# Hourglass attention with a GELU feed-forward layer: from batch 3 on, each head's 64 features on 64 partitions for the scores

## The chip, the cores and the metric

The kernel runs on one core of a Trainium2 chip. The metric is the device time of one execution in microseconds (us); lower is better. The time before the change is the median of three runs. The trace comes from one further, profiled execution.

The engines are named as in the profile: PE is TensorE (matrix products, with PEld for its weight loads), DVE is VectorE, ACT is ScalarE, POOL is GpSimd, SP is SyncE, whose queue here issues transfers only.

## The reference

Inputs `q`, `k`, `v` have the shape (8 batches, 8 heads, 576 tokens, 64 features); `w_in` is 512 x 2048 and `w_out` 2048 x 512. All are float32, and so is the output of 4608 x 512.

```python
# attention: B, H, S, D = 8, 8, 576, 64; factor = 4; Sd = 144
q_d, k_d, v_d = means over 4 neighbouring tokens          # (B, H, Sd, D)
out_d = softmax(q_d @ k_d.T / sqrt(D)) @ v_d
out_up = np.repeat(out_d, 4, axis=2)
mask = np.abs(pos[:, None] - pos[None, :]) < 4             # a band of 7 tokens
scores = np.where(mask, q @ k.T / sqrt(D), -1e9)
out_local = softmax(scores) @ v
x = (out_up + out_local).transpose(0, 2, 1, 3).reshape(B * S, H * D)
# feed-forward layer
h = x @ w_in
g = h * (1.0 / (1.0 + np.exp(-1.702 * h)))
return (g @ w_out).astype(np.float32)
```

## The kernel before, in words

**Two interleaved programs.** The feed-forward layer works on nine groups of 512 tokens. For group `g`, `mm1` makes 16 blocks of 128 hidden features (`hps_mm`, L712, four matmuls of 512 columns each) and ACT applies Silu to each (L723). `mm2` makes four blocks of 128 tokens by 512 outputs (L776, 16 matmuls each), ACT copies each into an `osb` buffer (L761) and SP stores it (L766). Batch `b = g + 1` goes through attention while group `g` runs; batch 0 is done before the groups, and groups 7 and 8 have no attention beside them.

**Positions.** The order of all engines is written out by hand. `attention(b)` returns six steps, and `POS = [13, 16, 35, 45, 56, 69]` says ahead of which block of `mm1` (0 to 15) or matmul of `mm2` (16 to 79, counted on from 16) each is put into the program. The steps are, for batches 2 to 7: the first scores on PE (13), their exponentials and masks (16), the second scores with exponentials and masks (35), the products with the values for head pairs 0 and 1 with their normalisation (`avn(0, 1)`, 45), `av_tr` (the same for pairs 2 and 3, and pair 0 turned back and merged, 56), and `tr(1, 2, 3)` (the other pairs turned back and merged, 69).

**Heads.** The eight heads are two quads `qd` (four heads) and four head pairs `hp`. One transfer per quad and name brings k or q as bfloat16 into `kb`, `qb` (L185, issued by POOL, two buffers each): head `r` of the quad lies on partitions 32r to 32r+31, 18 tokens to a partition. `prep_1` (L262) turns it on DVE in 32x32 blocks of 4-byte words, that is, of pairs of features: in `kT`, `qT` head `r` keeps its 32 partitions, and the pair's two features lie side by side in the last index `a`. A dot product over 64 features is thus two matmuls over 32 partitions, `a = 0` and `a = 1`, summed in PSUM.

**Scores.** `scores_mixed` makes the local scores in blocks of 64 keys by 60 queries: five chunks `i`, two halves `par`, four heads, two `a`, that is 80 matmuls (`score`, L360). The scores of the means (`score_d`, L372) are 24 matmuls of 144 columns. Their operands `kdT`, `qdT` are sums over four tokens that POOL makes in two steps (`pool_qk`, L292 and L296). ACT takes the exponentials (`exp_local` L410, `exp_down` L416), and DVE multiplies the local ones by the band's mask (`mask_local`, L424). `mask_local` comes behind the batch's preparation in DVE's order, and in the same order as the steps.

**Values.** SP loads the values twice, as rows (`load_v` into `vf`, one buffer) and as groups of four rows (`load_v4` into `v4`, one buffer). POOL casts the first (`prep_v`, L302) and sums the second (`prep_v4`, L308 and L311). The results `vbs` and `vds` have two buffers, one for odd and one for even batches.

**After the scores.** `av` makes 40 matmuls for a head pair (`av_local` L441 with 64x64 tiles, `av_down` L463), `normalise` divides by the sums on DVE (L479, L480), `transp` turns the result on PE (L494, L504), ACT spreads the part of the means (`copy_od`, L618), and DVE adds both into `xT` (`merge`, L639 and L645). The next group's first matmuls read `xT`.

**PSUM.** Three tiles `PA` go round: a score stage takes three, `avn(0, 1)` two, `av_tr` three, `tr(1, 2, 3)` three; the next group's first block takes one. Two tiles `PM` serve the feed-forward layer.

**Preparation.** At the head of each group, L904 to L935 put the work for batch `b` on the queues. For groups 1 to 6 that is, on DVE, four transposes; on POOL, the sums of quad 0, the loads of batch `b + 1`'s k and q, the cast of the values, the sums of quad 1, and the sums of the values; on SP, `load_v4(b)` and `load_v(b + 1)`.

Of the kernel before, what the change touches and what calls it, by code (L numbers as in the profile page):

```python
# [19 lines left out]
def kernel(  # L20
# [43 lines left out]
    eds = [persist.tile([128, 2, 480], BF16, name=f"ed{i}") for i in range(2)]  # L64
    v4 = persist.tile([128, 3, HP, 4 * D], FP32, name="v4")
    kdT = [persist.tile([128, 160, 2], BF16, name=f"kdT{i}") for i in range(NQ)]

    PA = [psum.tile([128, 2, 512], FP32, name=f"pa{i}") for i in range(3)]
    PM = [psum.tile([128, 512], FP32, name=f"pm{i}") for i in range(2)]
# [10 lines left out]
        return PM[turn["m"] % 2]  # L80

    wz = consts.tile([128, 512], BF16, name="wz")
    wf = consts.tile([128, 512], FP32, name="wf")
    off = consts.tile([128, 60], BF16, name="off")
    psel = consts.tile([128, 7, 64], BF16, name="psel")

# [24 lines left out]
    def fill():  # L111
        nc.vector.memset(wz, 0.0)
        nc.vector.memset(wf, 0.0)
        for t in kdT:
            nc.vector.memset(t[:, SD:160, :], 0.0)
        for t in vbs:
            nc.vector.memset(t[:, :, :, 64:65], 1.0)
        for t in vds:
            nc.vector.memset(t[:, :, :, 64:65], 4.0)
        for t in es:  # L120
            nc.vector.memset(t[:, :, 300:304], 1.0)
        for t in eds:
            nc.vector.memset(t[:, :, 432:480], 1.0)
# [56 lines left out]

    def load_1(name, src, store, b, qd):
        t = ldp.tile(
            [128, 1152], BF16, name=f"{name}b{qd}", tag=f"{name}b{qd}", bufs=2
        )
        nc.gpsimd.dma_start(  # L185
            out=t,
            in_=bass.AP(
                tensor=src.tensor, offset=src[b, 4 * qd].offset,
                ap=[[1152, 128], [1, 1152]],
            ),  # L190
        )
        store[b, qd] = t
# [75 lines left out]
    def prep_qk(b, qd):  # L268
        prep_1("k", b, qd)
        prep_1("q", b, qd)  # L270

    def new_qdT(b, qd):
        t = work.tile([128, SD, 2], BF16, name=f"qdT{qd}", tag=f"qdT{qd}", bufs=1)
# [115 lines left out]
    def scores_d(b, qd, sd):  # L389
# [3 lines left out]
                    score_d(b, qd, sd, kc, a, r)  # L393
        return sd

    def scores_mixed(b, qd):
        sp, sd = [ps_tile(), ps_tile()], ps_tile()
        for i in range(5):
            for a in range(2):
                if i >= 2:  # L400
                    for r in range(4):
                        score_d(b, qd, sd, i - 2, a, r)
                for x in (1, 0):
                    for r in range(4):
                        score(b, qd, sp, i, a, r % 2 if x == 0 else 1 - r % 2, r)
        return sp, sd
# [254 lines left out]
    def attention(b, slots=None):  # L661
        st = {}

        def s_pe(qd):
            st["s", qd], st["d", qd] = scores_mixed(b, qd)

        def s_act(qd):
            if qd == 0:
                nc.scalar.preload_act_table_set("exp_and_others")
            exp_local(qd, st["s", qd])  # L670
            exp_down(qd, st["d", qd])
            if qd == 1:
                nc.scalar.preload_act_table_set("silu_and_others")
            mask_local(qd)

        def s1():
            s_pe(1)
            s_act(1)

        def avn(*hps):  # L680
            def f():
                for hp in hps:
                    st["o", hp] = av(b, hp, slots and slots[hp % 2])
                for hp in hps:
# [24 lines left out]
        return first + [av_tr, tr(1, 2, 3)]  # L709

    def hps_mm(g, ffc, dmc, acc):
# [190 lines left out]
    for g in range(n_groups):  # L902
        b = g + 1
        if g == 0:  # L904
# [14 lines left out]
            nc.gpsimd.memset(v4[32:64], 0.0)  # L919
            load_v(2, gate=after(w_out_bf[0:1, 12, 0:1], nc.gpsimd))  # L920
            load_v4(2)
        elif b < B:
            if b > 2:
                load_v4(b)
            prep_qk(b, 0)
            pool_qk(b, 0)
            if b + 1 < B:
                for qd in range(NQ):
                    load_qk(b + 1, qd)
            prep_v(b, nc.gpsimd)  # L930
            if b + 1 < B:
                load_v(b + 1)
            prep_qk(b, 1)
            pool_qk(b, 1)
            prep_v4(b, nc.gpsimd)  # L935
        steps = {}
        if b < B:
            for n, f in zip(POS if g else POS_0, attention(b, None if g else (1, 2))):
# [36 lines left out]
```

## Time and profile before

| What | Value |
|---|---|
| Time, median of 3 runs | 323.0 us (322.31 to 323.63) |
| Time of the profiled execution | 320.42 us |
| Its span, first to last instruction | 318.6 us |
| Granted TensorE clock | 1.00 |
| Matmuls of the feed-forward layer, L712 and L776, busy | 139.2 and 128.7 us |
| Matmuls of the scores, L360 and L372 | 1280 of 197 ns and 384 of 230 ns |
| Weight loads of the scores, L360 | 1280 of 104 ns |
| DVE, transposes L262 | 32, 39.8 us |
| POOL, sums L292 and L296 of one name and quad | 1.15 and 0.67 us |
| POOL, one step of the value sums L308 and L311 | 1.33 and 0.76 us |
| DVE waiting for ACT ahead of the masks | 89.1 us in 14 places, the longest 12.6 us |
| POOL waiting for DVE's transposes | 84.7 us in 6 places, the longest 15.8 us |

The span is what the trace holds; the profiled execution's own time has 1.8 us around it. A duration in the trace is that of one instruction, and matmuls overlap: what a stage of matmuls takes is read from where it begins and where the next stage begins. A wait of an engine that is not the bound costs nothing by itself.

The order of POOL's and DVE's work in the group that begins at 128.24 us, with times from the span's start: DVE ends the merges of batch 3 at 129.07 and turns k and q until 133.5; POOL's sums run from 130.32, its four load issues from 134.00, the cast from 136.13, and the sums of the values from 142.15 to 148.6. The first scores begin on PE at 139.55, the second at 147.45, and the first products with the values at 150.69; the last step ends at 158.71, and the next group begins at 161.10.

### The profile page before, as it was taken

What the parts mean: (1) busy time and instruction counts of PE and PEld (TensorE: products, weight loads), DVE (VectorE), ACT (ScalarE), POOL (GpSimd) and SP (SyncE); (2) the same over time, 40 slices, a digit from 0 to 9 for tenths busy, and PEclk for the clock granted to TensorE, in tenths of its full rate; (3) what the DMA queues carried; (4) which work ended last, traced back from release to release, by engine and by line L of the source; (5) the groups of instructions that cost most, each with busy time, mean ns of one, the idle gap of its engine ahead of it and who ended that gap; (6) DMA issues with size and microseconds to landing.
All of it is one profiled execution on the core that took longest, in us unless ns stands there. A gap on an engine that the chain in (4) does not pass through costs nothing.

```text
span 318.6 us, 10993 instructions
## 1 busy us (share of the span) xinstructions
PE 309.5 (97%) x4927; PEld 156.9 (49%) x4927; DVE 133.6 (42%) x222; ACT 184.0 (58%) x314; POOL 138.9 (44%) x168
## 2 busy tenths in 40 slices
PE   7899999999999989999999999999999999999995
PEld 4465455444554545455545554455445544444444
DVE  6963825730684066703780378027811650000000
ACT  4464773577647674658465846674667556415611
POOL 8843782099209930696049703980297000000000
PEclk9999999999999999999999999999999999999999
DMA  7999999999719941598259915991360110020011
GB/s 121 116 191 209 184 90 207 185 270 230 180 39 218 199 114 70 144 216 173 71 134 206 188 41 136 206 205 58 109 107 2 71 68 2 0 99 33 2 65 67
DMA packets 64078, 40.02 MB, mean 126 GB/s; under 512 B 44064, under 2 KB 55456, under 8 KB 64032
## 3 DMA queue, kind: packets, MB, share of 16 engines
q0 software_dynamic: 19392, 14.95, 33.3%
q1 hardware_dynamic: 44496, 24.32, 32.7%
q8 instruction: 38, 0.62, 0.9%
q10 hardware_dynamic: 144, 0.07, 0.1%
q14 instruction: 8, 0.07, 0.1%
HBM read 44.83 MB, written 9.44 MB: 170 GB/s over the span
## 4 chain that ended last, share of the span: by engine, by line
PE 86%; DMA 7%; POOL 4%; issue 1%; ACT 0%; DVE 0%; POOLq 0%
PE pm L776 37%; PE pm L712 33%; DMA kb<-in_k_dram 5%; PE pa L360 3%; PE pa L776 2%; DMA qb<-in_q_dram 2%; PE pa L441 2%; PE pa L712 2%; PE pa L494 2%; PE pa L372 2%; PE pa L463 2%; PE pm L791 1%; POOL w_in_bf L238 1%; POOL vb L216 1%; POOL pq L292 1%
## 5 line engine op out<-in xcount | busy, mean ns | idle before, releaser
L776 PE MATMUL pm<-w_out_bf,gT 128*128 128x512 bf16 x528 | 120.8, 380 | 0.4 <-issue 0.4
L712 PE MATMUL pm<-xT,w_in_bf 128*128 128x512 bf16 x512 | 119.2, 379 | 0.0
L723 ACT ACTIVATE gT<-pm 128x512 bf16<-128x512 f32 x128 | 76.3, 598 | 44.7 <-PE pm L712 44.7
L712 PEld LDWEIGHTS <-w_in_bf 128*128 128x128 bf16 x576 | 55.6, 98 | 66.2
L776 PEld LDWEIGHTS <-gT 128*128 128x128 bf16 x560 | 52.0, 98 | 60.8 <-issue 1.7
L424 DVE TENSOR_TENSOR es<-es,mask 128x600 bf16<-128x600 bf16 x28 | 18.6, 667 | 90.1 <-ACT es L410 89.1
L292 POOL TENSOR_TENSOR pq<-kT 128x576 f32<-128x576 bf16 x13 | 15.1, 1159 | 84.7 <-DVE kT L262 84.7
L761 ACT ACTIVATE osb<-pm 128x512 f32<-128x512 f32 (+2 forms) x35 | 20.5, 586 | 38.3 <-PE pm L776 34.2
L618 ACT COPY od<-pa 128x384 f32<-128x384 f32 (+1 forms) x56 | 19.0, 406 | 26.4 <-PE pa L504 23.3
L480 DVE TENSOR_TENSOR y<-pa,rc 128x896 bf16<-128x896 f32 x28 | 30.6, 1092 | 1.0
L410 ACT ACTIVATE es<-pa 128x600 bf16<-128x600 f32 x32 | 19.7, 668 | 10.8 <-PE pa L360 10.6
L639 DVE TENSOR_TENSOR xT<-pa,od 128x570 bf16<-128x570 f32 x28 | 21.0, 752 | 8.0 <-ACT od L618 8.0
L308 POOL TENSOR_TENSOR v<-v 112x512 f32<-112x512 f32 x18 | 23.9, 1330 | 0.0
L763 DVE TENSOR_SCALAR osb<-pm 128x128 f32<-128x128 f32 x1 | 0.3, 293 | 55.0 <-ACT osb L761 55.0
L262 DVE STREAM_TRANSPOSE kT<-kb 128x576 f32<-128x576 f32 x16 | 20.0, 1248 | 5.6 <-DMA kb<-in_k_dram 5.5
L262 DVE STREAM_TRANSPOSE qT<-qb 128x576 f32<-128x576 f32 x16 | 19.8, 1240 | 0.8 <-DMA qb<-in_q_dram 0.6
L712 PE MATMUL pa<-xT,w_in_bf 128*128 128x512 bf16 x64 | 20.0, 379 | 0.0
L360 PEld LDWEIGHTS <-kT 32*64 32x64 bf16 x1280 | 14.7, 104 | 7.8 <-issue 6.6
L360 PE MATMUL pa<-qT,kT 32*64 32x60 bf16 x1280 | 17.2, 198 | 1.3 <-DVE qT L262 1.3
L216 POOL DMA_DIRECT2D vb<-in_v_dram x20 | 13.7, 699 | 8.1 <-DMA w_in_bf<-in_moe_w_in_dram 3.6
L292 POOL TENSOR_TENSOR pq<-qT 128x576 f32<-128x576 bf16 x13 | 14.9, 1147 | 0.0
L416 ACT ACTIVATE ed<-pa 128x864 bf16<-128x864 f32 x16 | 14.3, 897 | 0.1
(92 smaller groups left out, 278.9 us busy)
## 6 DMA issues: line engine op xcount, KB each, us to landing
out_dram<-osb SPq DMA_DIRECT2D x35, 256.0 KB, 2.1
vf<-in_v_dram SPq DMA_DIRECT2D x60, 128.0 KB, 5.3
v<-in_v_dram SPq DMA_DIRECT2D x36, 192.0 KB, 4.5
kb<-in_k_dram POOLq DMA_DIRECT2D x16, 288.0 KB, 6.5
qb<-in_q_dram POOLq DMA_DIRECT2D x16, 288.0 KB, 7.9
w_in_bf<-in_moe_w_in_dram POOLq DMA_DIRECT2D x4, 512.0 KB, 12.1
w_out_bf<-in_moe_w_out_dram POOLq DMA_DIRECT2D x4, 512.0 KB, 8.7
vb<-in_v_dram POOLq DMA_DIRECT2D x20, 64.0 KB, 5.7
```

Source lines behind the costliest of these rows:

```text
L262: nc.vector.transpose(out=t32.rearrange("p (i c) -> p c i", c=18), in_=store[b, qd].bitcast(FP32).rearrange("p (c d) -> p c d", c=18),)
L292: nc.gpsimd.tensor_tensor(out=t1, in0=sv[:, :, 0:2, :], in1=sv[:, :, 2:4, :], op=ALU.add)
L308: eng.tensor_tensor(out=t1[0:112], in0=x[:, :, 0:2, :], in1=x[:, :, 2:4, :], op=ALU.add)
L360: nc.tensor.matmul(sp[r // 2][64 * par : 64 * par + 64, r % 2, 60 * i : 60 * i + 60], lhsT=kT[b, qd][rows, k0 : k0 + 64, a], rhs=qT[b, qd] ...
L410: nc.scalar.activation(out=es[2 * qd + u][:, :, 0:300], in_=sp[u][:, :, 0:300], func=AF.Exp, scale=inv_sqrt_d,)
L480: nc.vector.tensor_tensor(out=y[:, xs], in0=ov[:, :, :, 0:D], in1=rc[:, xs].to_broadcast([128, n, 7, D]), op=ALU.mult,)
L618: nc.scalar.copy(out=od[:, 4 * t0 : 4 * (t0 + n)].rearrange("p (t f) -> p t f", f=4), in_=x[:, xx, 288 : 288 + n, None].to_broadcast([128, ...
L639: eng.tensor_tensor(out=sub(xT[hp], t0 + 3, (57, 2), (114, 5), (1, 57)), in0=sub(x, 3, (509, 2), (57, 5), (1, 57)), in1=sub(od, 3, (57, 2) ...
L712: nc.tensor.matmul(acc, lhsT=w_in_bf[:, dmc, ffc * 128 : (ffc + 1) * 128], rhs=xT[dmc][:, g * TG : g * TG + TG], start=(dmc == 0), stop=(d ...
L723: nc.scalar.activation(out=gT[:, ffc, :], in_=acc, func=AF.Silu, scale=GELU_SCALE)
L761: eng.activation(out=osb, in_=ap, func=AF.Copy, scale=1.0 / GELU_SCALE)
L776: nc.tensor.matmul(ops[t], lhsT=gT[:, ffc, t * 128 : (t + 1) * 128], rhs=w_out_bf[:, ffc, :], start=(ffc == 0), stop=(ffc == n_ffc - 1),)
```

## The change

From batch 3 on (`WIDE = 3`), the scores use a different layout. `turn2` turns k or q in 32x32 blocks of 2-byte elements, so that features 0 to 31 and 32 to 63 of a head lie in two planes `a` on the same 32 partitions. `widen` then moves 32-partition blocks with five copies on DVE: one saves plane 1 of all heads, and four put the two planes of each head onto 64 adjacent partitions (heads 0 and 2 of a quad in plane 0, heads 1 and 3 in plane 1). `pool_wide` sums over four tokens on POOL as before. `scores_wide` makes the scores with one matmul over 64 partitions in place of two over 32: 40 local ones and 12 of the means for each quad.

`attention` of these batches has `avn(0, 1)` ahead of the second scores, with its own positions `POS_W`. At the head of the groups, the values of batches 3 to 7 are prepared one batch ahead on POOL, and SP loads them first; `prep_wide` puts the transposes, the copies, the sums and the loads of the next batch's k and q in turn. In group 1 (batch 2), the cast and the sums of the values go from POOL to DVE, the loads of quad 1 for batch 3 come behind quad 1's transposes, and the values of batch 3 are prepared on POOL at the end.

The loads of k and q have one buffer in place of two, for all batches, and the constant `wf` lies in `v4`, which is not yet in use at that point.

```diff
+    kdW = [persist.tile([128, 2, 160], BF16, name=f"kdW{i}") for i in range(NQ)]
+    qdW = [persist.tile([128, 2, SD], BF16, name=f"qdW{i}") for i in range(NQ)]
+    kW = [persist.tile([128, 2, S], BF16, name=f"kW{i}") for i in range(NQ)]
+    qW = [persist.tile([128, 2, S], BF16, name=f"qW{i}") for i in range(NQ)]
+    WIDE = 3
...
-    wf = consts.tile([128, 512], FP32, name="wf")
+    wf = v4.rearrange("p k h c -> p (k h c)")[:, 0:512]
...
+        for t in kdW:
+            nc.vector.memset(t[:, :, SD:160], 0.0)
...
-            [128, 1152], BF16, name=f"{name}b{qd}", tag=f"{name}b{qd}", bufs=2
+            [128, 1152], BF16, name=f"{name}b{qd}", tag=f"{name}b{qd}", bufs=1
...
+    def turn2(name, b, qd):
+        store, dst = (kf, kW) if name == "k" else (qf, qW)
+        nc.vector.transpose(
+            out=dst[qd].rearrange("p a (i c) -> p c a i", c=18),
+            in_=store[b, qd].rearrange("p (c a d) -> p c a d", c=18, a=2),
+        )
+
+    def widen(name, b, qd):
+        w = (kW if name == "k" else qW)[qd]
+        half = work.tile([128, S], BF16, name="half", tag="half", bufs=1)
+        nc.vector.tensor_copy(out=half, in_=w[:, 1, :])
+        for s in range(2):
+            lo, hi = slice(64 * s, 64 * s + 32), slice(64 * s + 32, 64 * s + 64)
+            nc.vector.tensor_copy(out=w[lo, 1, :], in_=w[hi, 0, :])
+            nc.vector.tensor_copy(out=w[hi, 0, :], in_=half[lo, :])
+
+    def pool_wide(name, qd):
+        src, dst = (kW[qd], kdW[qd][:, :, 0:SD]) if name == "k" else (qW[qd], qdW[qd])
+        sv = src.rearrange("p x (j f) -> p (x j) f", f=4)
+        t1 = work.tile([128, 2, SD, 2], FP32, name="pq", tag="pq")
+        nc.gpsimd.tensor_tensor(
+            out=t1.rearrange("p x j f -> p (x j) f"),
+            in0=sv[:, :, 0:2], in1=sv[:, :, 2:4], op=ALU.add,
+        )
+        nc.gpsimd.tensor_tensor(
+            out=dst, in0=t1[:, :, :, 0], in1=t1[:, :, :, 1], op=ALU.add
+        )
+
+    def prep_wide(b):
+        def turn_load(name, qd):
+            turn2(name, b, qd)
+            if b + 1 < B:
+                load_1(name, *((k, kf) if name == "k" else (q, qf)), b + 1, qd)
+
+        def finish(name, qd):
+            widen(name, b, qd)
+            pool_wide(name, qd)
+
+        turn_load("k", 0)
+        finish("k", 0)
+        turn_load("q", 0)
+        turn_load("k", 1)
+        finish("q", 0)
+        turn_load("q", 1)
+        finish("k", 1)
+        finish("q", 1)
...
+    def scores_wide(qd):
+        sp, sd = [ps_tile(), ps_tile()], ps_tile()
+        for i in range(5):
+            for x in range(2):
+                for s in range(2):
+                    rows = slice(64 * s, 64 * s + 64)
+                    for par in range(2):
+                        k0 = 114 * i + KSTART[par]
+                        q0 = 114 * i + QSTART[par]
+                        nc.tensor.matmul(
+                            sp[s][64 * par : 64 * par + 64, x, 60 * i : 60 * i + 60],
+                            lhsT=kW[qd][rows, x, k0 : k0 + 64],
+                            rhs=qW[qd][rows, x, q0 : q0 + 60],
+                            start=True, stop=True,
+                            tile_position=(64 * s, 64 * par),
+                        )
+            if 1 <= i < 4:
+                kc = i - 1
+                for s in range(2):
+                    rows = slice(64 * s, 64 * s + 64)
+                    for x in range(2):
+                        nc.tensor.matmul(
+                            sd[64 * x : 64 * x + 64, s, SD * kc : SD * kc + SD],
+                            lhsT=kdW[qd][rows, x, 48 * kc : 48 * kc + 64],
+                            rhs=qdW[qd][rows, x, :],
+                            start=True, stop=True,
+                            tile_position=(64 * s, 64 * x),
+                        )
+        return sp, sd
+
     def scores_mixed(b, qd):
+        if b >= WIDE:
+            return scores_wide(qd)
...
+        if b >= WIDE:
+            first = first[:2] + [avn(0, 1), s1]
         return first + [av_tr, tr(1, 2, 3)]
...
     POS = [13, 16, 35, 45, 56, 69]
+    POS_W = [13, 16, 35, 46, 59, 71]
...
-        elif b < B:
-            if b > 2:
-                load_v4(b)
+        elif b < WIDE:
             prep_qk(b, 0)
             pool_qk(b, 0)
-            if b + 1 < B:
-                for qd in range(NQ):
-                    load_qk(b + 1, qd)
-            prep_v(b, nc.gpsimd)
+            load_qk(b + 1, 0)
+            prep_qk(b, 1)
+            load_qk(b + 1, 1)
+            prep_v(b, nc.vector)
+            load_v(b + 1)
+            prep_v4(b, nc.vector)
+            load_v4(b + 1)
+            pool_qk(b, 1)
+            if b + 1 == WIDE:
+                prep_v(b + 1, nc.gpsimd)
+                prep_v4(b + 1, nc.gpsimd)
+        elif b < B:
             if b + 1 < B:
                 load_v(b + 1)
-            prep_qk(b, 1)
-            pool_qk(b, 1)
-            prep_v4(b, nc.gpsimd)
+                load_v4(b + 1)
+            prep_wide(b)
+            if b + 1 < B:
+                prep_v(b + 1, nc.gpsimd)
+                prep_v4(b + 1, nc.gpsimd)
```

The step lists take `POS_W` in place of `POS` from batch 3 on.

More of the change, by code (lines that the diff above doesn't have):

```diff
@@ L921 @@
             load_v4(2)
-        elif b < B:
-            if b > 2:
-                load_v4(b)
+        elif b < WIDE:
             prep_qk(b, 0)
             pool_qk(b, 0)
-            if b + 1 < B:
-                for qd in range(NQ):
-                    load_qk(b + 1, qd)
-            prep_v(b, nc.gpsimd)
+            load_qk(b + 1, 0)
[10 more added lines that the diff above has]
+        elif b < B:
             if b + 1 < B:
                 load_v(b + 1)
-            prep_qk(b, 1)
-            pool_qk(b, 1)
-            prep_v4(b, nc.gpsimd)
+                load_v4(b + 1)
[3 more added lines that the diff above has]
+                prep_v4(b + 1, nc.gpsimd)
         steps = {}
         if b < B:
-            for n, f in zip(POS if g else POS_0, attention(b, None if g else (1, 2))):
+            for n, f in zip(POS_W if b >= WIDE else POS if g else POS_0, attention(b, None if g else (1, 2))):
                 steps.setdefault(n, []).append(f)
```

## The prediction

> **What bounds the kernel now.** I read the engines' busy time and the chain of waits first, then the windows of one group with attention and one without.
>
> ```profile
> PE 309.5 (97%) x4927; PEld 156.9 (49%) x4927; DVE 133.6 (42%) x222; ACT 184.0 (58%) x314; POOL 138.9 (44%) x168
> ...
> PE 86%; DMA 7%; POOL 4%; issue 1%; ACT 0%; DVE 0%; POOLq 0%
> ...
> 128.24:161.10 32.86, 32.86 (x602) 16.59 (x601) 15.90 (x25) 21.02 (x36) 17.75 (x19) 1.00 0.67 147
> ...
> 260.00:287.60 27.60, 27.60 (x130) 12.52 (x129) 0.72 (x2) 11.83 (x20) 0.00 (x0) 1.00 0.10 39
> ```
>
> TensorE is the bound: 97% busy, 86% of the chain, clock 1.00. A group with attention (first window; columns are length, then busy us of PE, PEld, DVE, ACT, POOL) takes 32.86 us, the group without 27.60: a batch's attention costs 5.3 us of PE. DVE has 17 us to spare there, POOL 15. So the change gains what it takes off PE, and loses what it makes PE wait.
>
> **Scores.** Batches 3 to 7 have ten score stages, each 104 matmuls now, 52 after. One present stage, and the 64-row matmuls nearest to the new ones (times are start, length):
>
> ```profile
> 147.44:148.43 0.99, 0.99 (x105) 0.94 (x105) 0.59 (x1) 0.43 (x1) 0.91 (x2) 1.00 0.94 183
> 150.69:151.51 0.82, 0.82 (x81) 0.78 (x81) 0.24 (x1) 0.82 (x1) 0.00 (x0) 1.00 0.05 15
> ...
> 150.69 0.23 PE L441 MATMUL pa<-vb,es 64*64 64x65 bf16 x4
> ...
> 150.69 0.35 PE L441 MATMUL pa<-vb,es 64*64 64x65 bf16 x20
> ...
> 47.68 0.99 PE L329 MATMUL pa<-vb,psel 128*64 128x256 bf16 x14
> ```
>
> Four 64x64 tiles run side by side: 16 more matmuls add 0.12 us, so a wave of four takes 0.03. The first-AV window has 20 waves in 0.82: at 0.030 to 0.035 each, 0.12 to 0.22 remains for entering and leaving. A new stage has 40 local matmuls, 10 waves, 0.30 to 0.35. Its 12 matmuls of 144 columns are 3 waves; L329 gives their price: 7 pairs of 256 columns in 0.99, one matmul lasting 0.28, so (0.99 - 0.28)/6 = 0.118 a pair, 0.46 ns a column, 0.066 a wave, 0.20 together. Sum 0.62 to 0.77; I take 0.69 against 0.99, **0.30 saved, 3.0 us in ten stages**. Bounds: half of the stage (5 us) if it goes by the count of matmuls; a loss of 1.5 if only two tiles of a wave overlap (20 x 0.033 + 6 x 0.066 + 0.12 = 1.18 a stage, 0.19 over), which the AV rows speak against.
>
> PE also pauses where the profile shows no cause: 0.93 us at 117.3 in the AV of batch 3, and 0.58 us over these ten stages beyond 0.98 each (1.10 in the stage at 139.55). With half as many instructions in the scores some of this should go: I take 0.5 of 1.5, bounds 0 and 1.5.
>
> **DVE's new preparation.** Per batch four transposes of 128x1152 2-byte elements replace four of 128x576 4-byte ones, and 20 copies are added (100 in all).
>
> ```profile
> L262 DVE STREAM_TRANSPOSE kT<-kb 128x576 f32<-128x576 f32 x16 | 20.0, 1248 | 5.6 <-DMA kb<-in_k_dram 5.5
> L639 DVE TENSOR_TENSOR xT<-pa,od 128x570 bf16<-128x570 f32 x28 | 21.0, 752 | 8.0 <-ACT od L618 8.0
> L645 DVE TENSOR_TENSOR xT<-pa,od 128x6 bf16<-128x6 f32 x28 | 4.7, 169 | 1.0
> L302 POOL CAST vb<-vf 128x2560 bf16<-128x2560 f32 x6 | 14.1, 2354 | 0.0
> ...
> 149.28 0.47 DVE L424 TENSOR_TENSOR es<-es,mask 128x600 bf16<-128x600 bf16 x1 [1.25 <-ACT es L410]
> ...
> 146.63 1.40 DVE L424 TENSOR_TENSOR es<-es,mask 128x600 bf16<-128x600 bf16 x1
> ...
> 146.20 1.49 POOL L308 TENSOR_TENSOR v<-v 112x512 f32<-112x512 f32 x1
> ```
>
> No row shows a 2-byte transpose. The same bytes give 1.25 us; as many elements in a microsecond would give 2.4, and one element a step (564 more in L639 than in L645 cost 0.583, 1.03 ns each) 1.35. I take 1.25, by bytes. No row shows a large DVE copy. L639 and L645 give 0.16 fixed and 7.7 input bytes a ns (two f32 streams); the free mask, two bf16 streams of 1200 B in 0.47, gives the same 7.7. A copy reads 1152 B: 0.16 + 0.15 = 0.31, with a 0.03 step to the next. Bounds: 0.17, L645's whole price, and 0.75, one element a step. I take 0.31, since two unlike rows agree on bytes. Five copies that wait on each other are 1.7, a batch 4 x 1.25 + 4 x 1.7 = 11.8 us against 4.5.
>
> Is that hidden? Let T0 be the start of a group (128.24). DVE is free at T0+0.8 now; the batch's last PE step comes two positions nearer to the group's end, so T0+1.2 then. k of the first four heads takes until 4.1, two transposes until 6.6, q's copies until 8.3, POOL's two sums (1.15 and 0.67) until 10.1. The first scores come at T0+11.3: hidden, by 1.2 us. All of DVE's preparation ends at T0+13, before the masks at 17.5. Of the waits on SBUF tiles this is the tightest; SP's loads and the kb/qb loads, which now wait for the transposes in a single buffer, come a whole group ahead of use.
>
> **First AV before the second scores.** AV stays at position 35 but loses the second scores as cover. All from now on starts 0.3 sooner against T0. The exps of the first scores end at T0+17.5 and 18.0 and a free mask takes 0.47, so the masks are ready at 18.0 and 18.5; head pair 0 starts at 18.9 and pair 1 at 19.3. But DVE and POOL meet here: the mask at 146.63 took 1.40 instead of 0.47, ending 0.33 after POOL's sum that began at 146.20. The second mask, done at 148.03, would thus be ready at T0+19.5, 0.2 late. Today nothing waits, since AV comes at 150.69. Behind it DVE's queue holds the normalisation, which the second scores' PSUM tiles wait for: AV start + 3.2 us (150.69 to 153.92), and 0.82 plus 11 matmuls of 0.216 bring those scores at + 3.2 too. I take a stall of **0.2 us a batch, 1.0 in all**; bounds 0 (POOL idle) and 1.4 (a 2.36 us cast between the masks). The later positions have slack: the second scores' exps end 2.8 after their start, av_tr comes 3.4 after it. At the group's end head pair 3's merge ends 0.46 before the matmul that needs it and loses 0.43: 0.05 a batch, 0.25 in all, bounds 0 and 2.
>
> [...]
>
> **Values and start-up.** In group 1 (61.4 to 94.3) DVE gets a cast of 2560 elements (0.16 + 2560 x 0.5 to 1.03 ns, 1.5 to 2.8 us) and six sums (512 and 256 elements: 0.69 and 0.42, 3.3 together): done by 73, while the masks come at 79; DVE's 12.5 us idle stretch hides it, and without that it would cost 6. Batch 3's values on POOL then wait for SP's loads, some 15 us from 68, and still end by 92, ahead of POOL's next work at 96. From group 2 on the values are made a batch early and SP loads them first, ahead of stores that are due 17 us later. Two pad memsets (0.1 each) fall into DVE's 1.1 us wait for POOL at 2.4; wf inside v4 is free of readers before POOL clears v4 at 47. At start-up the second kb/qb loads wait for transposes that end at 12.4, while POOL issues them at 16.4. All zero; bound +1.
>
> **Sum.** -3.0 - 0.5 + 1.0 + 0.25 = -2.3 us: the span of 318.6 becomes 316.3. The profiled run took 320.4, the median of the runs is 323.0, 4.4 above the span; the same difference gives **320.7**. With stages of 0.62, no pause left and no stall it is -5.2, 317.8.
>
> **Rivals.** (a) *The masks wait for POOL's cast*, and the kernel is slower. Each batch POOL now runs from about T0+13 with no pause: 3.7 us of sums, a cast of 2.36, six sums of 6.3 together, to T0+25, and both masks fall in there. A cast that slips between them ends the second at T0+20.7, a stall of 1.4: 7 in five batches, -3.5 + 7 + 0.25 gives 326.8. It decides from 0.65 a batch. For: five of the seven first mask pairs show such a wait now, and the cast is the longest of POOL's operations. Against: with sums of 0.7 to 1.3 between them the stall is 0 to 0.3, and pair 0's work covers 0.4.
> (b) *The copies meet POOL too.* If a copy also has to wait for a POOL instruction and the reverse, as the masks do, I get, laying both queues out by these durations, q pooled at T0+11.3, the last sums at 19, the second mask at 19.5 to 19.8: 0.35 to 0.9 a batch, 321.5 to 324.3. [...] For: the mask rows. [...]
> (c) *The preparation is late.* At 0.75 a copy, q is ready at T0+12.7 and pooled at 14.5, and the masks queue behind copies until 21.8: about 3.3 a batch, 336. With 2.4 us transposes: 3 a batch, 334. Against: bytes agree in two rows.
> (d) *The scores do not shrink*, because two row groups overlap worse than four: +1.5 + 0.75 gives 325.3. Against: the AV waves.
>
> **Chances.** Forecast 0.52 (with its own range 318 to 321.9); (a) 0.17; (b) 0.17; (c) 0.09; (d) 0.05. Half a per cent, 1.6 us, is about what a measurement of this kernel can tell from no change. Faster: most of the forecast and a little of (b), 0.53. Same: the forecast's upper end and about half of (b), 0.15. Slower: (a), (c), (d) and the rest of (b), 0.32. The range runs from 317.5 to 328; it leaves out (c) and some of the tails.
>
> **What would show it.** Score stages of 0.6 to 0.8 us on PE with 52 matmuls; copies near 0.31 and transposes near 1.25; q's copies ending by T0+9; the first masks ending by T0+19.6, PE idle before L441 of 0.2 or less. A stall of over 0.65 there, or PE waiting for q at the first scores, makes the prediction wrong.

## The result and the profile after

The changed kernel takes 377.2 us (median of 4 runs, 376.16 to 380.63) against 322.65 for the kernel before on the same chip: ratio 1.176 [1.171, 1.182]. The forecast was 320.7. The profiled execution has a span of 375.2 us at a granted clock of 0.93, 56.6 us more than before.

From the profile's page: the engines' busy time, the chain by engine, and three of the costliest groups (instructions, then busy us and mean ns of one, then the idle time ahead of them and what ended it):

```profile
PE 320.5 (85%) x4407; PEld 158.9 (42%) x4407; DVE 257.5 (69%) x331; ACT 183.6 (49%) x314; POOL 135.8 (36%) x161
...
PE 62%; DVE 25%; POOL 5%; issue 4%; DMA 1%; ACT 1%; ACTq 0%; POOLq 0%; DVEq 0%
...
L281 DVE STREAM_TRANSPOSE kW<-kb 128x1152 bf16<-128x1152 bf16 x10 | 52.0, 5197 | 0.0
L281 DVE STREAM_TRANSPOSE qW<-qb 128x1152 bf16<-128x1152 bf16 x10 | 51.2, 5117 | 0.4
L459 PE MATMUL pa<-qW,kW 64*64 64x60 bf16 x400 | 10.8, 216 | 36.3 <-DVE qW L293 36.3
```

PE has 520 matmuls fewer, but its share fell from 97% to 85%. DVE, 0% of the chain before, now holds a quarter of it. One 2-byte transpose takes 5.12 us where the forecast has 1.25. The timeline of a group (start, length) shows what waits for it; PE begins the group at 138.53, DVE its preparation at 139.71:

```profile
139.71 5.12 DVE L281 STREAM_TRANSPOSE kW<-kb 128x1152 bf16<-128x1152 bf16 x1
144.86 0.31 DVE L289 COPY half<-kW 128x576 bf16<-128x576 bf16 x1
...
146.66 5.12 DVE L281 STREAM_TRANSPOSE qW<-qb 128x1152 bf16<-128x1152 bf16 x1
...
151.43 5.28 DVE L281 STREAM_TRANSPOSE kW<-kb 128x1152 bf16<-128x1152 bf16 x1
...
157.56 0.26 PE L459 MATMUL pa<-qW,kW 64*64 64x60 bf16 x2 [7.62 <-DVE qW L293]
157.88 0.30 DVE L293 COPY qW<-half 32x576 bf16<-32x576 bf16 x1
158.23 0.42 PE L459 MATMUL pa<-qW,kW 64*64 64x60 bf16 x14 [0.41 <-DVE qW L293]
158.26 1.14 POOL L299 TENSOR_TENSOR pq<-qW 128x576 f32<-128x576 bf16 x1 [0.63 <-DVE qW L293]
...
160.20 0.34 PE L471 MATMUL pa<-qdW,kdW 64*64 64x144 bf16 x4 [1.55 <-POOL qdW L303]
```

The order is the one written out by hand: q's turn, then the second k's turn, and only then q's copies. With three transposes ahead, q is complete at 158.18, some 8.4 us after PE has come to the first scores (149.77 at full speed, an estimate: 61 matmuls of 0.216 after 136.58). The forecast has q ready 3 us ahead of them. PE stands for 7.6 us, and 1.6 more until POOL has q's sums. The windows of the same stretch (length, busy us of PE, PEld, DVE, ACT, POOL, then granted clock, DMA share, GB/s), with the second score stage as the last row:

```profile
149.56:157.56 8.00, 0.38 (x3) 0.10 (x2) 7.90 (x6) 0.75 (x2) 1.12 (x2) 0.84 1.09 199
157.56:161.03 3.47, 1.50 (x52) 1.18 (x52) 3.40 (x3) 0.00 (x0) 1.88 (x3) 0.50 0.61 92
161.03:165.30 4.27, 4.27 (x18) 1.56 (x12) 4.08 (x8) 1.19 (x2) 1.06 (x2) 0.52 0.15 10
173.15:173.78 0.63, 0.63 (x54) 0.59 (x53) 0.00 (x0) 0.00 (x0) 0.55 (x2) 1.00 0.00 0
```

The wait has a second price: from 154.93 on, still within it, the clock is granted at half, in the score stage and in some ten matmuls behind it, which follow each other at 427 ns instead of 216. The stretch to the first AV thus takes 8.8 us (161.03 to 169.85) where the same 31 matmuls take 6.8 in the kernel before (140.65 to 147.44): 2 us a batch. The last row is the stage as the change meant it: **0.63 us, where the kernel before has 0.98.**

The waits add up (us in total, times, longest):

```profile
PE pa L459 <- DVE qW L293: 36.3, 10, 7.6
PE pa L471 <- POOL qdW L303: 7.9, 5, 1.7
```

These 44.2, 11 us of half clock (some 52 more matmuls at 427 ns than before, 0.211 each), 4.4 in the five first score stages (1.51 each with their waits taken off, against 0.63: at half clock, and in three pieces) and 0.9 for a PE pause of 1.9 us in group 1 where the kernel before has one of 0.9 in group 2, less 4.1 for ten stages of 0.63 (the ten take 10.4 before), make 56.4 of the 56.6.

### The profile page after: what moved, and what is told of

It reads as the page before. It is cut to its first block, busy times and chain, and to the rows that moved or that the text cites. A ratio compares the mean times of both kernels' runs of the same rounds, so it can differ in the third digit from the quotient of the medians.

```text
span 375.2 us, 10089 instructions
## 1 busy us (share of the span) xinstructions
PE 320.5 (85%) x4407; PEld 158.9 (42%) x4407; DVE 257.5 (69%) x331; ACT 183.6 (49%) x314; POOL 135.8 (36%) x161
## 4 chain that ended last, share of the span: by engine, by line
PE 62%; DVE 25%; POOL 5%; issue 4%; DMA 1%; ACT 1%; ACTq 0%; POOLq 0%; DVEq 0%
PE pm L864 28%; PE pm L800 19%; DVE kW L281 13%; DVE qW L281 5%; PE pa L800 3%; PE pa L864 2%; DVE xT L725 2%; PE pa L527 2%; POOL vb L223 2%; POOL pq L299 2%; DMA vb<-in_v_dram 1%; PE pa L549 1%; PE pa L580 1%; ACT od L704 1%; PE pa L471 1%
## 5 line engine op out<-in xcount | busy, mean ns | idle before, releaser
L800 PE MATMUL pm<-xT,w_in_bf 128*128 128x512 bf16 x512 | 129.3, 403 | 0.0
L281 DVE STREAM_TRANSPOSE kW<-kb 128x1152 bf16<-128x1152 bf16 x10 | 52.0, 5197 | 0.0
L281 DVE STREAM_TRANSPOSE qW<-qb 128x1152 bf16<-128x1152 bf16 x10 | 51.2, 5117 | 0.4
L459 PE MATMUL pa<-qW,kW 64*64 64x60 bf16 x400 | 10.8, 216 | 36.3 <-DVE qW L293 36.3
L192 POOL DMA_DIRECT2D kb<-in_k_dram x16 | 9.4, 587 | 56.5 <-DVE kW L281 38.3
L459 PEld LDWEIGHTS <-kW 64*64 64x64 bf16 x400 | 9.1, 128 | 41.0 <-issue 41.0
L725 DVE TENSOR_TENSOR xT<-pa,od 128x570 bf16<-128x570 f32 x28 | 21.0, 751 | 7.1 <-ACT od L704 7.1
L299 POOL TENSOR_TENSOR pq<-kW 128x576 f32<-128x576 bf16 x10 | 12.0, 1202 | 23.3 <-DVE kW L293 23.3
L362 POOL TENSOR_TENSOR v<-v 112x512 f32<-112x512 f32 x15 | 19.9, 1326 | 0.0
L192 POOL DMA_DIRECT2D qb<-in_q_dram x16 | 9.2, 574 | 29.0 <-DVE qW L281 14.1
L299 POOL TENSOR_TENSOR pq<-qW 128x576 f32<-128x576 bf16 x10 | 11.4, 1143 | 16.7 <-DVE qW L293 16.7
```

What stands on the lines that cost most here:

```text
L281: nc.vector.transpose(out=dst[qd].rearrange("p a (i c) -> p c a i", c=18), in_=store[b, qd].rearrange("p (c a d) -> p c a d", c=18, a=2),)
L299: nc.gpsimd.tensor_tensor(out=t1.rearrange("p x j f -> p (x j) f"), in0=sv[:, :, 0:2], in1=sv[:, :, 2:4], op=ALU.add,)
L362: eng.tensor_tensor(out=t1[0:112], in0=x[:, :, 0:2, :], in1=x[:, :, 2:4, :], op=ALU.add)
L459: nc.tensor.matmul(sp[s][64 * par : 64 * par + 64, x, 60 * i : 60 * i + 60], lhsT=kW[qd][rows, x, k0 : k0 + 64], rhs=qW[qd][rows, x, q0 : ...
L725: eng.tensor_tensor(out=sub(xT[hp], t0 + 3, (57, 2), (114, 5), (1, 57)), in0=sub(x, 3, (509, 2), (57, 5), (1, 57)), in1=sub(od, 3, (57, 2) ...
L800: nc.tensor.matmul(acc, lhsT=w_in_bf[:, dmc, ffc * 128 : (ffc + 1) * 128], rhs=xT[dmc][:, g * TG : g * TG + TG], start=(dmc == 0), stop=(d ...
```

## The experiments

Ratios are to the kernel before, timed beside each run on the same chip (its median lay between 320.06 and 321.01, lower than the 323.0 that the forecast started from).

**e1_words: the price of the transpose alone.** 4-byte words in place of 2-byte elements, all else as in the changed kernel. The copies then leave k and q in the wrong places, so this kernel does not compute the reference; e2_rows, e4 and e5 do not either.

```diff
-            out=dst[qd].rearrange("p a (i c) -> p c a i", c=18),
-            in_=store[b, qd].rearrange("p (c a d) -> p c a d", c=18, a=2),
+            out=dst[qd].rearrange("p a t -> p (a t)").bitcast(FP32).rearrange("p (i c) -> p c i", c=18),
+            in_=store[b, qd].bitcast(FP32).rearrange("p (c d) -> p c d", c=18),
```

> The changed kernel with one edit: turn2 moves the same bytes as 576 words of 4 bytes, as prep_1 does, so that k and q lie wrong in kW and qW (pairs of features side by side, tokens mixed); the scores are not the reference's, every instruction count and size behind the transposes is the same. Theory: the slowdown of 54 us comes from the price of a 2-byte transpose alone (5.12 us against 1.25), through DVE to the first scores; then transposes take 1.25 here, no wait for q at the first scores, and the time is that of the forecast, 318 to 322. [...] Rival, that order, waits or the granted clock cost by themselves: over 330.

320.63 us, ratio 0.9966 [0.9937, 0.9995]. The transposes take 1.25 us, and the waits for q and its sums are gone. A group takes 32.05 us (first scores to first scores) against 32.86. All of the loss thus hangs on this price. From batch 2's first scores to the end the profiled execution takes 242.8 us against 246.1: 3.3 less. But its start-up ends 2.3 later than in the kernel before; whether that is so in all runs is not settled. The ratio is worth 1.1 us only, and the medians, 320.63 against 320.38, show no gain.

**e2_rows: what makes it dear.** Still 2-byte elements, but each 32 results side by side, not 36 bytes apart.

```diff
-            out=dst[qd].rearrange("p a (i c) -> p c a i", c=18),
+            out=dst[qd].rearrange("p a (c i) -> p c a i", i=32),
```

> The changed kernel with one edit: the 2-byte transposes write each block's 32 results side by side (64 bytes) instead of 36 bytes apart, so the tokens of a head lie in another order in kW and qW and the local scores are not the reference's. If the price is that of scattered 2-byte writes, a transpose falls from 5.12 us to 1.2 to 1.4 and the time to that of e1_words. If it is that of a 2-byte block, whatever is written where, it stays at 5.1 and the time at 377. In between (2.4): 334 or so.

320.81 us, ratio 0.9999 [0.9968, 1.0029]; the transposes take 1.37 us. What is dear is not the 2-byte transpose but writing 2-byte results far apart. This run also shows the mask stall of the forecast's rival (a), and e1_words the same place without it. First e2_rows, then e1_words, from the timelines:

```profile
146.31 2.32 POOL L356 CAST vb<-vf 128x2560 bf16<-128x2560 f32 x1
146.84 2.50 DVE L510 TENSOR_TENSOR es<-es,mask 128x600 bf16<-128x600 bf16 x2 [2.44 <-ACT es L496]
149.01 0.35 PE L527 MATMUL pa<-vb,es 64*64 64x65 bf16 x20 [0.72 <-DVE es L510]
```

```profile
146.71 1.03 DVE L512 TENSOR_TENSOR es<-es,mask 128x600 bf16<-128x600 bf16 x2 [3.12 <-ACT es L498]
...
148.55 2.32 POOL L358 CAST vb<-vf 128x2560 bf16<-128x2560 f32 x1 [2.99 <-DMA v<-in_v_dram]
```

Where POOL's cast starts half a us ahead of the masks, these take 2.50 instead of 1.03 and PE stands 0.6 to 0.7 us, in three of five batches. Where the cast still waits for its load, nothing happens.

**e3_forms and e6_spread: the operations by themselves.** The kernel before, with transposes and copies of many forms on DVE in group 7, where DVE is nearly idle (0.72 of 27.60 us busy before).

> The kernel before, with single DVE instructions added while DVE and POOL have nothing to do (group 7), each form twice, on tiles that nobody reads any more. 4-byte transposes, results 72 bytes apart: 1.25 us as before; side by side: 0.75 if the scattering costs, 1.25 if not. 2-byte transposes, results 36 bytes apart: 5.1; side by side in two layouts: 1.35 if the scattering costs, 5.1 if the block does; 4 bytes apart: between; half as many blocks, 36 bytes apart: half of 5.1. Copies of 576 elements read 4 bytes apart: 0.46 to 0.75; 1152 of them: 0.75 to 1.35; 32 partitions read and written 4 bytes apart: 0.46 to 0.75; side by side: 0.31. The time as before.

> The kernel before with DVE forms added in group 7, each twice, all of 512 elements. 2-byte transposes with results 2, 4, 8, 16 and 36 bytes apart: 0.70, 0.73 and, if the price grows with the number of 64-byte or larger pieces written, steps towards 2.3 (512 of 5.1/1152); if it jumps at one distance, the distance shows. 4-byte transposes with results 4, 8, 16 and 72 bytes apart: 0.70 to 1.12. A plain copy that writes 2-byte elements 36 bytes apart: 0.70 if only the transpose pays for scattered writes, 2.3 if every DVE write does; one that reads them 36 bytes apart and writes side by side: 0.43 to 0.70; side by side both: 0.30.

The groups of e3_forms (mean ns last):

```profile
L723 DVE STREAM_TRANSPOSE kT<-kb 128x1152 bf16<-128x1152 bf16 x2 | 10.2, 5114 | 0.1
L729 DVE STREAM_TRANSPOSE kT<-kb 128x1152 bf16<-128x1152 bf16 x2 | 2.9, 1472 | 0.1
...
L725 DVE STREAM_TRANSPOSE kT<-kb 128x1152 bf16<-128x1152 bf16 x2 | 2.8, 1379 | 0.1
L719 DVE STREAM_TRANSPOSE kT<-kb 128x576 f32<-128x576 f32 x2 | 2.5, 1252 | 0.0
L721 DVE STREAM_TRANSPOSE kT<-kb 128x576 f32<-128x576 f32 x2 | 1.6, 778 | 0.1
```

L723 is the changed kernel's transpose, results 36 bytes apart; L729 writes them 4 bytes apart, L725 side by side. L719 is the kernel before's, words 72 bytes apart, and L721 words side by side: the 1.25 us of before, which the forecast read as a price by bytes, already held a price for scattered writing. (The form of 576 elements named in the expectation as 36 bytes apart was in fact written side by side: 0.78 us.) Six groups of e6_spread, 512 elements each:

```profile
L730 DVE STREAM_TRANSPOSE v<-kb 128x512 bf16<-128x512 bf16 x2 | 4.9, 2462 | 0.1
L728 DVE STREAM_TRANSPOSE v<-kb 128x512 bf16<-128x512 bf16 x2 | 2.7, 1326 | 0.1
L742 DVE COPY v<-kb 128x512 bf16<-128x512 bf16 x2 | 2.5, 1271 | 0.1
...
L726 DVE STREAM_TRANSPOSE v<-kb 128x512 bf16<-128x512 bf16 x2 | 1.5, 754 | 0.1
L724 DVE STREAM_TRANSPOSE v<-kb 128x512 bf16<-128x512 bf16 x2 | 1.4, 711 | 0.0
...
L746 DVE COPY qT<-kb 128x512 bf16<-128x512 bf16 x2 | 0.6, 294 | 0.1
```

Transposes with results 2, 4, 8 and 16 bytes apart (L724, L726, L728, L730) take 0.71, 0.75, 1.33 and 2.46 us; at 36 bytes it is 2.38, no more. A plain copy that writes 36 bytes apart takes 1.27 us, side by side 0.29 (L742, L746). The larger price is thus that of the writes; a copy that only reads 36 bytes apart takes 0.65.

**e4_words_old_order: first AV ahead of the second scores or not.** e1_words with the old order and positions.

```diff
-            first = first[:2] + [avn(0, 1), s1]
+            pass
-    POS_W = [13, 16, 35, 46, 59, 71]
+    POS_W = [13, 16, 35, 45, 56, 69]
```

> e1_words with the old order and positions from batch 3 on (second scores at 35, first AV at 45, 56, 69); the output is as wrong as there. It tells what the first AV ahead of the second scores is worth once the transposes are cheap. If it is needed because the second quad's sums come late (at T0+19 against second scores at T0+18.9): 1 to 3 us slower than e1_words, with PE idle before the second scores. If the masks wait for POOL in e1_words, this one is up to 3 us faster, with PE never idle before the first AV. Forecast: within 1 us of e1_words.

320.61 us, ratio 0.9993 [0.9967, 1.0019], against e1_words' 0.9966 [0.9937, 0.9995]. The intervals overlap, and the medians are alike (320.61 and 320.63): no effect of the order is clear of the noise.

**e5_gate: POOL's next values behind the first masks.** e1_words, with a one-element copy on POOL that reads the masked scores.

```diff
+        nc.gpsimd.tensor_copy(out=gate[0:1], in_=es[1][0:1, 1, 299:300])
+        prep_v(b, nc.gpsimd)
+        prep_v4(b, nc.gpsimd)
```

> e1_words (4-byte transposes, so k and q lie wrong and the scores are not the reference's) with one more edit: POOL's cast and sums of the next batch's values wait, by a one-element copy, for the batch's first masks, instead of running into them. Theory: in e1_words PE idles 0.7 to 0.8 us ahead of the first AV in batches 3, 4 and 5 because the second mask waits for POOL; then the masks take 0.47 each here, the first AV never waits, and the time is 2 to 2.5 us under e1_words, 0.988 to 0.993 of before. Rival, the first AV waits for something else (exponentials, PSUM): the 0.7 stays. Rival, the delayed values come late for something: up to 2 us slower.

319.03 us, ratio 0.9965 [0.9943, 0.9987], the same as e1_words. The expectation started from a wrong reading: the waits of 0.6 to 0.7 us ahead of the first AV are in e2_rows' trace, and e1_words' has none. Where the cast comes behind the masks anyway, the gate has nothing to win; what it would win in e2_rows was not tried.

**e7_swap: the change with cheap transposes.** Words are turned, features stay in pairs of 2-byte elements, and the copies swap elements in place; q's copies come ahead of the second k, and the gate of e5_gate is in.

```diff
-        nc.vector.tensor_copy(out=half, in_=w[:, 1, :])
+        nc.vector.tensor_copy(out=half, in_=w[:, :, 1])
...
-            nc.vector.tensor_copy(out=w[lo, 1, :], in_=w[hi, 0, :])
+            nc.vector.tensor_copy(out=w[lo, :, 1], in_=w[hi, :, 0])
```

> A version that computes the reference: 4-byte transposes as before batch 3, then the same five copies on the pairs in place (2-byte elements read and written 4 bytes apart, 0.46 to 0.48 by e3_forms), q's copies ahead of the second quad's first transpose, and the values behind the first masks as in e5_gate. DVE's preparation is 4 x (1.25 + 2.55) = 15.2 us a batch against 11.8 in e1_words. q is ready at T0+9.9 and pooled at 11.7 to 12.4 against scores at 11.3: 0.3 to 1.0 lost a batch at the scores of the means; preparation ends at T0+16.4 to 18.4: 0 to 1 lost at the masks. Against 3.5 gained: 0.99 to 1.005 of before. If the copies meet POOL more than in e1_words, 1.005 to 1.015.

321.01 us, ratio 1.0028 [0.9998, 1.0057]: not faster than before. A copy over elements 4 bytes apart takes 0.48 instead of 0.30, and PE waits 0.3 to 0.4 us for the masks in four groups. The larger item is a PE pause of 2.27 us in group 1 at 92.65, with seven matmuls at half clock behind it. (The expectations below count pauses from the start of one matmul to the start of the next, 0.19 more: 2.46.) The changed kernel has one there too (1.86), and so has e2_rows (2.27). Group 1's attention has no wide scores, so this is another part of the change.

**e8_narrow: the change without wide scores.** What is left: group 1's values on DVE, all values a batch early, one buffer for each load of k and q, `wf` in `v4`.

```diff
-            prep_wide(b)
+            prep_qk(b, 0)
+            pool_qk(b, 0)
...
+            prep_qk(b, 1)
+            pool_qk(b, 1)
```

> The changed kernel without wide scores, transposes and copies and with the old order and positions: left are group 1's values on VectorE, the values of batches 3 to 7 one batch early, the single buffers and wf in v4. It computes the reference. Theory: these cost nothing, 0.997 to 1.003 of before. Rival: one of them costs by itself (the second buffers, loads in another place): 1.005 or more, with a wait of DVE for kb or of POOL for vf that before does not have.

323.63 us, ratio 1.0109 [1.0065, 1.0154]. The parts that the forecast put at nothing cost about 1.1% (four runs). In the profiled execution, 5.2 us longer than the kernel before's, it is mainly in one place, from the timeline of PE:

```profile
90.77 0.27 PE L578 MATMUL pa<-id,y 60*64 60x60 bf16 x10
94.02 0.32 PE L578 MATMUL pa<-id,y 60*64 60x57 bf16 x8 [2.97 <-issue]
94.10 0.32 PE L588 MATMUL pa<-id,y 48*64 48x48 bf16 x6
94.36 1.89 PE L860 MATMUL pm<-w_out_bf,gT 128*128 128x512 bf16 x4
```

PE stops in the middle of a burst of transposes and waits for no other engine; 13 matmuls at 427 ns follow (2.7 us). The transfers tell more. In the kernel before the ten loads of batch 3's plain values and the six of its pooled ones are 12 us apart; here they leave back to back, and the DMA engines are full from 86 to 93 us (busy for 0.8 or more in 38 of 40 slices). A 16 KB block of queue q8, which the DMA view calls "instruction", landed at 89.87 us in the kernel before, and at 92.56 here. I take these blocks for PE's code: there are 38 in the kernel before and here, and 34 in the changed kernel, which has 520 matmuls and 520 weight loads fewer.

**e9_loads_back: the loads apart.** e8_narrow with the six loads back at the start of group 2.

```diff
-            load_v4(b + 1)
+            if b + 1 < WIDE:
+                load_v4(b + 1)
...
+            if b == WIDE:
+                load_v4(b)
```

> e8_narrow with one thing put back: the six loads of batch 3's pooled values are issued in group 2, as in the kernel before, and not in group 1 behind the ten loads of its plain values; their sums on POOL move to group 2 with them. Theory: in e8_narrow the 16 loads of values fill the DMA engines from 85 to 93 us (17 windows of the DMA row at 9), the 16 KB block of PE's instructions that lands at 88 to 89 us in the kernel before lands at 91 to 92 there, PE stands 3.2 us in the middle of a burst of transposes and then runs some 13 matmuls at half clock (2.7 us). With the loads back the gap of 3.17 us and the half clock behind it go, the profile shows no PE gap over 1.3 us between 85 and 97 us, and the time is 3 to 6 us under e8_narrow's 323.6: 317.6 to 320.6, ratio to the kernel before 0.982 to 1.000. Rival: the cost of e8_narrow is that of the single buffers or of values prepared a batch early in the later groups; then the time stays at 322.5 to 324 and the ratio over 1.005, whether or not the gap goes.

321.42 us, ratio 1.0041 [1.0013, 1.0070]: 2.2 us better than e8_narrow by the ratios, short of the expected 3. The pause of group 1 is gone (0.5 us is left at 86.8), but the edit made another row of loads: the six moved ones now go out just ahead of batch 4's ten and six, which e8_narrow has back to back too, from 95 to 117 us in all, and behind them PE pauses 0.8 us at 117.0 and 1.8 us at 121.6, with some seven matmuls at half clock. The pause went with the loads.

**e10_swap_loads_back and e11_swap_old_values: two tries to have both.** e7_swap with those loads back in group 2, and e7_swap with all steps of the values where the kernel before has them:

```diff
         finish("q", 0)
+        prep_v(b, nc.gpsimd)
+        if b + 1 < B:
+            load_v(b + 1)
+        prep_v4(b, nc.gpsimd)
         turn_load("k", 1)
```

> e7_swap (wide scores from word transposes and a swap of the 2-byte elements; the values behind the first masks) with the same six loads put back in group 2. Theory: e7_swap's gap of 2.46 us at 92 us and the seven matmuls at half clock behind it (1.5 us) go, the shorter score stages are left, and the time is 3 to 4 us under e7_swap's 321.0: 317.0 to 318.5, ratio to the kernel before 0.983 to 0.995, faster than both kernels. Rival: what e7_swap gives back lies in groups 3 to 6 (second scores that wait some 0.5 us for the later preparation), and the time stays within 1 us of 321.0, ratio 0.998 to 1.006.

> e7_swap with every step of the values where the kernel before has it: group 1's on POOL, each batch's in its own group, their loads in the two old places (pooled values at the group's start, plain ones behind POOL's cast); no gate. On POOL the cast and the pooled values stand between the sums of q of the first pair of heads and those of k of the second. What is left of the change is the wide scores with their preparation and one buffer for each load of q and k. Theory: PE's pauses in e7_swap, e8_narrow and e9_loads_back end 1.3 to 1.6 us after a 16 KB block of its instructions has landed, and the block is late where the ten loads of plain values and the six of pooled ones go out back to back; with the loads apart there is no pause over 1.2 us between 84 and 130 us and no matmuls at 427 ns, and the ten shorter score stages (0.33 us each, 3.3 us) are left less some 0.5 us for each of the later groups' stalls: 317.5 to 319.5, ratio to the kernel before 0.985 to 0.998. Rival: the single buffers, or masks that meet POOL's later sums, eat it: 320 to 322, ratio 0.999 to 1.006.

Both forecasts of the time failed, though in both runs PE's pause at 92 us is gone as expected. e10: 326.84 us, ratio 1.0193 [1.0156, 1.0229]. In batch 3 POOL makes the pooled values behind four sums of q and k that wait for DVE's copies, and the first AV stands for them (2.7, 1.8 and 1.8 us, ended by POOL's sums L366). e11: 359.89 us, ratio 1.1236 [1.1203, 1.1269]. Its timeline of DVE and POOL in the group whose preparation begins at 135.59:

```profile
145.68 2.32 POOL L361 CAST vb<-vf 128x2560 bf16<-128x2560 f32 x1
...
145.97 2.34 DVE L291 COPY half<-kW 128x576 bf16<-128x576 bf16 x1
...
147.96 1.48 POOL L367 TENSOR_TENSOR v<-v 112x512 f32<-112x512 f32 x1
148.34 1.43 DVE L294 COPY kW<-kW 32x576 bf16<-32x576 bf16 x1
149.51 0.83 POOL L370 TENSOR_TENSOR vd<-v 112x256 bf16<-112x256 f32 x1
149.81 0.87 DVE L295 COPY kW<-half 32x576 bf16<-32x576 bf16 x1
```

Each copy, 0.48 by itself, ends 0.3 us after a POOL instruction has ended, and POOL's are longer too (1.48 against 1.27). Nine copies run in step with POOL, the masks queue behind them, and PE waits 32.1 us for masks in all. This is the meeting of copies and POOL that the forecast's rival (b) feared: making POOL's values a batch early is what keeps them apart.

**e12_before_early_v4: the loads alone.** The kernel before with one edit, the six loads in group 1 instead of group 2.

> The kernel before with one edit: the six loads of batch 3's pooled values are issued in group 1, right behind the ten of its plain values, and not at the start of group 2. Every other instruction is as before. Theory (loads back to back delay PE's code): the profile has a PE pause of 1 to 3 us between 86 and 96 us that ends 1.3 to 1.6 us after a 16 KB instruction block has landed, where the kernel before has none; if the pause passes some 2 us, matmuls at 427 ns stand behind it (1.5 to 2.7 us more). Time 321.5 to 326, ratio to the kernel before 1.003 to 1.017. Rival: the pause in group 1 comes from DVE's values or the single buffers of the changed kernel; then no new pause is seen and the time is within 0.7 us of before, ratio 0.998 to 1.002.

323.17 us, ratio 1.0057 [1.0019, 1.0095]. Nothing else differs, and PE pauses at the same point of the same burst:

```profile
91.23 0.27 PE L494 MATMUL pa<-id,y 60*64 60x60 bf16 x10
92.95 0.25 PE L494 MATMUL pa<-id,y 60*64 60x57 bf16 x8 [1.45 <-issue]
```

In the DMA view the 16 KB block is at 90.62 to 91.70, between loads that keep the engines full (98% from 90 to 91 for queue q1 alone). In this run, e7_swap, e8_narrow, e9_loads_back, the changed kernel and the kernel before (its pause at 117.3), PE goes on 1.25 to 1.61 us after a block has landed (1.79 in one shorter pause of e7_swap). Moving loads alone thus brings the pause, and its end follows the code: the "issue" here is a wait for code, as far as these traces tell. How long it gets is not set by the loads alone. e1_words, e4 and e5 issue the same 16 loads back to back and pause 0.75, 1.17 and 0.60 us in group 1, without half clock behind it, and each figure is from one profiled execution. e12's 0.6% is also less than e8_narrow's 1.1%; what the single buffers and DVE's values cost by themselves was not measured.

## Why the prediction was wrong

- **The step that failed is the transpose's price**, "I take 1.25, by bytes": 5.12 us measured, because its results are written 36 bytes apart. The other readings, 1.35 and 2.4, were far off too: they went by bytes or by elements, and none looked at how far apart the results go. Before (L719) and after (L723) both scatter; the new form writes twice as many results, at twice the price for each (4.4 against 2.2 ns). Rival (c), the late preparation, is what happened, at 377 instead of 334 to 336. e1_words and e2_rows show it: with transposes of 1.25 and 1.37 us the time is 320.6 and 320.8, where the forecast was 320.7. That agreement is luck in part: the forecast took 2.3 us off a kernel of 323.0, while these two ran beside one of 320.4 and gained 1.1 us and nothing by their ratios. The gain in the scores, larger than forecast, was lost again; the points below name costs that the traces show, but do not add up to it one by one.
- **Scores**: 0.69 predicted, 0.63 measured, 0.35 saved a stage. The bound of the AV rows held; 3.5 us in ten stages instead of 3.0. Rival (d) is out.
- **Copies**: 0.31 predicted, 0.30 measured where POOL is still. Beside POOL up to 1.1 in e1_words and 2.34 in e11: copies wait for POOL's instructions as rival (b) feared. In e1_words this cost no wait of PE that the trace shows, in e11 32 us of them.
- **First AV ahead of the second scores**: a stall of 0.2 a batch predicted. It is 0.6 to 0.7 where POOL's cast comes first, else 0 (e2_rows, e1_words): rival (a) in part, in three of five batches. The order itself shows no effect (e4). The loss of 0.05 a batch at the group's end is not seen: e1_words' groups are 0.8 us shorter, all that the two stages give.
- **PE's pauses**: 0.5 us less predicted; they are not fewer with fewer matmuls. e1_words still has one of 0.97 us at 217.4. The longer ones (1.45 us in e12, 2.97 in e8_narrow) come where a code block landed late (91.70 and 92.56 us, 89.87 before), and move with the loads.
- **Values, start-up, single buffers**, "all zero; bound +1": 1.1% with narrow scores (e8). The forecast laid out SP's loads against the stores and the values' due times, but not against PE's code, which landed later where loads filled the DMA engines (at 91.70 us in e12, 89.87 before).
- **Half clock**: not in the forecast at all. Each of the changed kernel's five long waits cost some 2 us more by it.

No version tried beats the kernel before while computing the reference. What would be wanted, q on 64 partitions without scattered writes, with the loads of the values spread out, was not found.

## What to carry to other kernels

Price an operation by its access pattern on both sides, not by its bytes (a copy of 512 elements took 0.29 us side by side, 0.65 read and 1.27 written 36 bytes apart): where the trace has no row with the same distance between results, the upper bound is open, and a factor of four was hidden here. A pause of PE that the profile calls "issue" is to be looked up in the DMA view, beside the code's queue: moving loads together can cost more than it hides (0.6% in e12). And a layout of DVE work that is dense in copies has to be kept clear of POOL's long instructions (0.48 us became up to 2.34 in e11).

## What the hardware showed that was not expected

- DVE's price for scattered 2-byte results rises with the distance up to 16 bytes and then stays: 1.4, 1.5, 2.6 and 4.8 ns an element at 2, 4, 8 and 16 bytes, 4.6 at 36 (e6_spread, by 512 elements). 4-byte words: 0.71 us for 512 at 4 and 8 bytes, 1.10 at 16, 1.14 at 72. The side-by-side forms of e3_forms differ by 1.04 ns an element (1379 ns for 1152, 778 for 576); with results 36 bytes apart it is 4.4 ns each (5114 for 1152).
- Matmuls of 64x64 tiles overlap so well that 52 of them end in 0.63 us, 12 ns each (the changed kernel, from 173.15).
- Whether half clock follows a pause is not set by its length alone. In the traces the granted clock changes only every 3.41 us or a multiple of it (in the changed kernel after 3.41, 6.83, 10.24, 17.07, 34.13 us and more). The windows below are such steps, first two of e7_swap, then two of e2_rows (there counted on from the first change, at 4.61). Both had the same pause of 2.27 us at the same place in the program, but e7_swap's lay in one step, and e2_rows' 1.54 and 0.73 us lay in two:

```profile
92.47:95.88 3.41, 1.14 (x39) 0.66 (x27) 1.75 (x4) 1.78 (x6) 3.25 (x4) 1.00 0.33 118
95.88:99.29 3.41, 3.41 (x10) 1.24 (x9) 3.11 (x6) 0.13 (x1) 1.24 (x2) 0.50 0.02 5
...
89.94:93.35 3.41, 1.87 (x70) 1.00 (x69) 2.04 (x6) 1.90 (x5) 3.25 (x5) 1.00 0.71 237
93.35:96.76 3.41, 2.68 (x26) 1.35 (x26) 2.23 (x5) 0.70 (x2) 1.83 (x2) 1.00 0.02 6
```

Half clock also came behind steps with 1.82 us of pause (e9_loads_back), 1.86 (the changed kernel's group 1) and 1.99 (e8_narrow), and not behind e12's 1.45. The limit is not sharp: one step of the changed kernel, from 107.14, has 1.89 us of idle time and full clock behind it. Some 7 matmuls of 512 columns run at 427 ns then, in e8_narrow 13.
